# Attention and two feed-forward layers on one core: float32 late scores for five pairs of heads, PSUM banks kept across the stages, and later steps for some loads and stores

## The chip, the cores and the metric

The kernel runs on one core of a Trainium2 chip. The metric is the device time of one execution in microseconds (us). The engines of the core are TensorE (PE in the profile, its weight loads PEld), VectorE (DVE), ScalarE (ACT), GpSimd (POOL) and SyncE (SP), which issues most of the DMAs.

## The reference

Shapes: q, k, v are (4, 8, 576, 64); the first layer is 512 to 2048 to 512, the second too; 2304 tokens.

```python
scores = scale * np.matmul(q, k.transpose(0, 1, 3, 2))     # scale = 1/8
mask = block_i >= block_j                                   # blocks of 64 positions
scores = np.where(mask, scores, -1000000000.0)
attn = softmax(scores)                                      # minus the row's maximum, 1e-9 in the sum
x = (attn @ v) as tokens x 512
h = x @ w_in;  g = np.maximum(h, 0.0) + alpha * np.minimum(h, 0.0);  x = g @ w_out     # first layer
h = x @ w_in2; g = np.where(h > 0.0, h, np.exp(np.minimum(h, 0.0)) - 1.0); out = g @ w_out2
```

The weights arrive as 64-bit floats and are turned into 32-bit ones on the core.

## The kernel before

**Attention** works on 16 pairs of heads, `n` = 0 to 15. A list `SEQ` of 64 slots sets the order: for the first eight pairs the early scores (query rows 0 to 255), one pair a slot, then for each of these pairs three late slots, `i` = 2, 3 and 4 (rows 256 to 383, 384 to 511, and the last 64), then the same for the other eight. Late slots of pairs 0 to 4 are slots 8 to 22. A slot `k` emits, each engine in program order: the scores on TensorE into one of two double banks (`twin`, called pair in the profile), products with v (`second`) and transposes of earlier slots, the row maxima on VectorE (line 319), the exponentials on ScalarE (line 346), and, two slots later, the division by the sums on GpSimd (line 96, tile `p`). The scores of slot `k` + 2 need the double bank of slot `k`, that is, its exponentials.

Early scores multiply float32 tiles as they were loaded (line 290). Late scores are three products of "fp32r" parts: `high_parts` (GpSimd: `qh`, `kh`, `kl`) and `low_parts` (VectorE: `ql`, line 270) split q and k into a high and a low part, and line 297 adds high x high, high x low and low x high. For `i` = 4 the last 64 query rows of both heads stand on the diagonal of a 128 x 128 tile `qdiag` (one for the high and one for the low parts, two sets), which `diagonal` fills by copies on GpSimd and ScalarE, and line 302 multiplies it by both heads' keys, 288 columns at a time.

`second(n, 1)` multiplies five chunks of v with the transposed probabilities `pt` (line 444). The fifth chunk has 64 rows of v, the others 128. Its closure `out` makes the high part of x on ScalarE (line 450) and the low part on VectorE (line 89), for the block of 256 rows and for the 64 tail rows (`xtail`).

**The weights** come by `load_w`: a DMA into `wraw` (three buffers), then, `arrival` ticks later, two steps on ScalarE (133, 134), three on VectorE (138, 139, 143), a word addition on GpSimd (148), a cast on ScalarE (162), a subtraction on VectorE (89, tile `w`). `later(t, f)` emits f after t ticks: a tick is a slot in attention, and half a step afterwards.

**The first layer beside attention** (`l1_beside`, lines 599 and 611) puts six products at a time between slots, for three units of 512 tokens. It borrows PSUM banks of the ring "t" that transposes and `second` use. After attention the steps `units` follow: per step one `f` of 16 columns blocks of the hidden layer, first layer A, B, D (lines 580 and 684), then the second, C (634 and 659). Units 0 to 3 have 512 tokens; unit 4, the 64-row tails of all pairs, has 256. `l1_gate` makes `neg` on ScalarE (557), `g` on VectorE (560), and its high and low parts on ScalarE (564) and GpSimd (89). After attention, all eight PSUM banks are one new pool: "h" takes banks 5, 6, 7, "acc" takes 0 to 4. x goes through DRAM (`xd`), and so does the first layer's output (`zd`, `yd`).

Of the kernel before, what the change touches and what calls it, by code (L numbers as in the profile page):

```python
# [9 lines left out]
F32 = mybir.dt.float32  # L10
# [31 lines left out]
def attention_moe_kernel(ctx: ExitStack, tc: tile.TileContext, qT, kT, v_a, v_b, w1, w2, alpha, out):  # L42
# [146 lines left out]

    att = ExitStack()  # L190
    ps = att.enter_context(pool("ps", 1, space=PSUM))
    twin = [ps.tile([P, 2, 512], F32, name=f"pair{i}") for i in range(2)]
    bank = [None] * 4 + [ps.tile([P, 512], F32, name=f"bank{i}") for i in range(4, 8)]
    ap1 = att.enter_context(pool("att1", 1))
    ap2 = att.enter_context(pool("att2", 2))
    vraws = [ap1.tile([P, 2, 5, D], F32, name=f"vraw{i}") for i in range(2)]

    qdiag = [[ap1.tile([P, P], F32R, name=f"qdiag{i}{k}") for k in range(2)] for i in range(2)]
# [39 lines left out]
    def load_early_v(d):  # L238
        b, hs = duo(d)
        v = vraws[d % 2].rearrange("p h c d -> p (h c d)")[:, :512].rearrange("p (h c d) -> p h c d", h=4, c=2)  # L240
        nc.sync.dma_start(out=v, in_=v_a[b, hs, :, :2, :].rearrange("h p c d -> p h c d"))
        for a in range(2):
            st[2 * d + a]["v"] = v[:, 2 * a:2 * a + 2]

# [7 lines left out]
    def load_late_v(n):  # L252
# [4 lines left out]
        nc.sync.dma_start(out=v[:64, :, 4, :], in_=v_b[b, hs].rearrange("e p d -> p e d"))  # L257

    def high_parts(n):
        s = st[n]  # L260
        q, k = s["raw"]
        for which, x, scale in (("q", q[:, :320], 0.125), ("k", k, None)):
            s[which] = [ap2.tile([P, x.shape[1]], F32R, tag=f"{which}{t}", name=f"{which}{t}") for t in "hl"]
            copy("p", s[which][0], x, scale)
        low_part("p", s["k"][1], k, s["k"][0])

    def low_parts(n):
        s = st[n]
        hi, lo = s["q"]
        dve.scalar_tensor_tensor(out=lo, in0=s["raw"][0][:, :320], scalar=0.125, in1=f32(hi), op0=ALU.mult, op1=ALU.subtract)  # L270

    def diagonal(n):
        for low in range(2):
            for x in range(2):
                r = slice(64 * x, 64 * x + 64)
                copy("pa"[low], qdiag[n % 2][low][r, r], f32(st[n]["q"][low])[r, 256:320])
# [4 lines left out]
    def scores(n, i):  # L281
        s = st[n]
        s["sb", i] = sb = twin[take("s")]
        if i < 4:
# [8 lines left out]
            q0, cols = P * i - 256, slice(0, P * (i + 1))  # L293
            for t, (qp, kp) in enumerate(PASSES):
                for x in range(2):
                    r = slice(64 * x, 64 * x + 64)
                    pe.matmul(sb[:, x, cols], s["q"][qp][r, q0:q0 + P], s["k"][kp][r, cols], start=t == 0, stop=t == 2)  # L297
        else:
            kn = S // 2
            for r in range(2):  # L300
                for t, (qp, kp) in enumerate(PASSES):
                    pe.matmul(sb[:, r, :kn], qdiag[n % 2][qp], s["k"][kp][:, kn * r:kn * (r + 1)],  # L302
                              start=t == 0, stop=t == 2)
# [60 lines left out]
    def transposes(n, i):  # L364
# [3 lines left out]
        if i in (EARLY, 2):  # L368
            s["pt"] = ap1.tile([P, 2, 1280], F32, tag=f"pt{n % 2}", name="pt")
        pt = s["pt"]  # L370
# [48 lines left out]
    def x_out(n, half):  # L419

        b, p = PAIRS[n]
        u = unit_of(n, half)
        if n % (2 * NPAIR) == 2 * NPAIR - 1:
            later(2, lambda: nc.sync.dma_start(out=xd[u], in_=f32(x1[u])))
        if half == 1:
            later(2, lambda: nc.sync.dma_start(out=xd[B][:, :, p, 64 * b:64 * b + 64], in_=f32(st[n]["tail"])))
# [4 lines left out]
    def second(n, half):  # L431
# [8 lines left out]
        for j in chunks:  # L440
            rows = 64 if j == 4 else P
            lo, o = max(0, P * j - q0), place(half, j)
            for x in range(2):
                pe.matmul(op[64 * x:64 * x + 64, lo:qn], s["v"][:rows, x, j, :], s["pt"][:rows, x, o + lo:o + qn],  # L444
                          start=j == 0, stop=j == chunks[-1], skip_group_check=True)
# [209 lines left out]
    def l2_y(u, f, gs):  # L655
        for tg in range(UNITS[u] // P):
# [4 lines left out]
            if f == NF - 1:  # L661
# [5 lines left out]
                else:  # L667
                    for k in range(2):
                        r = S * (2 * tg + k) + 512
                        nc.sync.dma_start(out=out[r:r + 64, :], in_=o[64 * k:64 * k + 64, :])  # L670

# [26 lines left out]
    with tc.manual_schedule(engines={ET.PE, ET.Activation, ET.DVE, ET.Pool, ET.SP}):  # L698
# [31 lines left out]
        for u, a, b, c, d in stretches:  # L730
            assert a >= X_DONE[u]
            parts = l1_beside(u)
            for first, end, n in ((a, b, 2 * FA), (c, d, 2 * KC)):
                slots(k, first)
                k = first
                for j in range(n):
                    next(parts)
                    to = first + (2 * (j + 1) * (end - first) + n) // (2 * n)
                    slots(k, to)
                    k = to  # L740
# [5 lines left out]
    with tc.manual_schedule(engines={ET.PE, ET.Activation, ET.DVE, ET.Pool, ET.SP}):  # L746
# [3 lines left out]
        ps = ctx.enter_context(pool("ps_all", 1, space=PSUM))  # L750
        bank[:] = [ps.tile([P, 512], F32, name=f"bank{i}") for i in range(8)]
        w_pools.append(ctx.enter_context(pool("w2", NF - 8)))
        late_pools.append(ctx.enter_context(pool("late", 1)))
        ring("h", 5, 6, 7)
        ring("acc", *range(5))
        units = [("A", 3), ("A", 4)] + [("B", u) for u in (2, 0, 1)] + [
# [13 lines left out]
        for i in range(len(steps) + lag):  # L770
            if i in w_at:
                arrival[0] = 6 if i < 6 else 4 if i < first_of["C", 2] - 4 else 2
                load_w(*w_at[i])
# [47 lines left out]
```

## Time and profile before

| | |
|---|---|
| median of three runs | 984.5 us (984.43 to 985.5) |
| the profiled execution | 985.47 us; first to last instruction 983.7 us |
| TensorE busy | 959.4 us (98%) |
| VectorE busy | 549.5 us (56%) |
| ScalarE busy | 438.4 us (45%) |
| GpSimd busy | 341.6 us (35%) |
| HBM traffic | 107 GB/s over the span |
| VectorE's first operation | starts at 3.69 us, when the first q has landed |
| one memset of 64 x 128 on VectorE | 0.17 us |

Busy is the union of an engine's instructions. What lies between the profiled execution's time and its span is before the first and after the last instruction. The busy share is a mean over stages that have different limits, so the stages have to be looked at one by one. In the views below a time at a row's start is in us from the first instruction; "idle" and square brackets name the time in which the engine did nothing just before, and what ended it.

### The profile page before, as it was taken

How to read it: one execution, taken by the hardware profiler on the slowest of the kernel's cores; microseconds unless marked ns; L12 is line 12 of the kernel's file. 1: busy time of each engine (PE TensorE's matmuls, PEld its weight loads, DVE VectorE, ACT ScalarE, POOL GpSimd, SP SyncE). 2: the span in 40 equal slices, each digit the busy share in tenths (PEclk: the TensorE clock that was granted, in tenths of full speed). 3: DMA queues.
4: the chain of work that ended last, by engine and by line, in shares of the span. 5: the costliest groups of instructions: out<-in, count | busy, mean ns of one | idle time of the engine just before them, and what ended most of it. 6: DMA issues, size and time to landing. Idle time of an engine off the chain costs nothing.

```text
span 983.7 us, 13873 instructions
## 1 busy us (share of the span) xinstructions
PE 959.4 (98%) x5064; PEld 779.2 (79%) x5064; DVE 549.5 (56%) x1012; ACT 438.4 (45%) x985; POOL 341.6 (35%) x401
## 2 busy tenths in 40 slices
PE   9888999999999999999999999999999999999997
PEld 7556666776789888888888888888888888888896
DVE  6999777775375454543554685994333332433343
ACT  6877787675354443433433553652222222222232
POOL 6888678664264343433443551330000000000000
PEclk9999999999999999999999999999999999999999
DMA  6553574432545522612537444322002100200010
GB/s 197 197 162 95 149 239 161 136 90 94 199 141 175 184 80 85 214 32 97 170 109 244 162 151 150 107 84 109 1 1 86 44 1 0 86 1 1 1 43 22
DMA packets 55524, 105.77 MB, mean 108 GB/s; under 512 B 11040, under 2 KB 29472, under 8 KB 54304
## 3 DMA queue, kind: packets, MB, share of 16 engines
q1 hardware_dynamic: 55168, 104.62, 32.2%
q8 instruction: 40, 0.66, 0.3%
q14 instruction: 28, 0.23, 0.1%
q10 hardware_dynamic: 288, 0.26, 0.1%
HBM read 76.55 MB, written 28.31 MB: 107 GB/s over the span
## 4 chain that ended last, share of the span: by engine, by line
PE 89%; DVE 5%; issue 2%; ACT 2%; POOL 1%; DMA 1%; SPq 0%; POOLq 0%; ACTq 0%; DVEq 0%
PE bank L634 20%; PE bank L659 20%; PE bank L580 16%; PE bank L684 16%; PE bank L444 4%; PE bank L611 3%; PE bank L599 2%; PE bank L384 2%; PE pair L297 1%; PE pair L290 1%; PE bank L377 1%; PE bank L207 1%; PE pair L302 1%; DVE wword L143 1%; DMA wraw<-w 1%
## 5 line engine op out<-in xcount | busy, mean ns | idle before, releaser
L634 PE MATMUL bank<-x,w 128*128 128x512 f32 (+1 forms) x960 | 210.0, 368 | 0.0
L634 PEld LDWEIGHTS bank<-x,w 128*128 128x128 f32 x960 | 169.4, 188 | 31.1
L580 PE MATMUL bank<-x,w 128*128 128x512 f32 (+1 forms) x816 | 175.5, 365 | 3.1 <-DVE g L560 1.9
L580 PEld LDWEIGHTS bank<-x,w 128*128 128x128 f32 x816 | 141.3, 189 | 27.9 <-DVE g L560 2.1
L560 DVE SCALAR_TENSOR_TENSOR g<-neg,beta,bank 128x512 f32<-128x512 f32 (+1 forms) x80 | 55.3, 692 | 130.5 <-ACT neg L557 130.4
L639 DVE TENSOR_SCALAR e<-e 128x512 f32<-128x512 f32 (+1 forms) x80 | 33.6, 420 | 165.5 <-ACT e L638 165.5
L148 POOL TENSOR_TENSOR wword<-wword,wraw 128x512 int32<-128x512 int32 x64 | 92.7, 1448 | 80.8 <-DVE wword L143 60.9
L638 ACT ACTIVATE e<-bank 128x512 f32<-128x512 f32 (+1 forms) x80 | 44.2, 552 | 168.5 <-PE bank L634 168.5
L659 PE MATMUL bank<-w,gs 128*128 128x512 f32 x432 | 104.7, 390 | 0.0
L659 PE MATMUL bank<-w,gsl 128*128 128x512 f32 x432 | 104.7, 390 | 0.0
L96 POOL TENSOR_SCALAR p<-p,stat 128x256 f32<-128x256 f32 (+4 forms) x144 | 85.0, 605 | 31.1 <-DVE stat L355 17.2
L659 PEld LDWEIGHTS bank<-w,gs 128*128 128x128 f32 x432 | 80.6, 188 | 16.3
L659 PEld LDWEIGHTS bank<-w,gsl 128*128 128x128 f32 x432 | 80.6, 188 | 16.3
L557 ACT ACTIVATE neg<-bank 128x512 f32<-128x512 f32 (+1 forms) x80 | 44.0, 550 | 102.6 <-PE bank L580 102.2
L89 POOL TENSOR_TENSOR gs<-g,gs 128x512 fp32r<-128x512 f32 (+1 forms) x46 | 56.5, 1229 | 94.8 <-ACT gs L564 94.8
L346 ACT ACTIVATE p<-pair,stat 128x256 f32<-128x256 f32 (+4 forms) x144 | 77.9, 551 | 24.5 <-DVE stat L319 18.9
L684 PE MATMUL bank<-gs,w 128*128 128x512 f32 (+1 forms) x408 | 87.8, 365 | 0.0
L684 PE MATMUL bank<-gsl,w 128*128 128x512 f32 (+1 forms) x408 | 87.8, 365 | 0.0
L684 PEld LDWEIGHTS bank<-gs,w 128*128 128x128 f32 x408 | 70.7, 189 | 12.2
L684 PEld LDWEIGHTS bank<-gsl,w 128*128 128x128 f32 x408 | 70.7, 189 | 12.2
L143 DVE SCALAR_TENSOR_TENSOR wword<-wraw,wword 128x512 uint32<-128x512 uint32 x64 | 74.3, 1161 | 2.2
L89 DVE TENSOR_TENSOR w<-wword,w 128x512 fp32r<-128x512 f32 x64 | 65.4, 1021 | 15.6 <-ACT w L162 15.4
(82 smaller groups left out, 1249.4 us busy)
## 6 DMA issues: line engine op xcount, KB each, us to landing
wraw<-w SPq DMA_DIRECT2D x64, 512.0 KB, 4.7
xd<-x SPq DMA_DIRECT2D x4, 2048.0 KB, 7.5
x<-xd SPq DMA_DIRECT2D x16, 512.0 KB, 7.0
x<-yd SPq DMA_DIRECT2D x4, 2048.0 KB, 9.5
vraw<-v_a SPq DMA_DIRECT2D x24, 256.0 KB, 3.6
kraw<-kT SPq DMA_DIRECT2D x16, 288.0 KB, 4.5
yd<-gs SPq DMA_DIRECT2D x8, 512.0 KB, 3.4
yd<-gsl SPq DMA_DIRECT2D x8, 512.0 KB, 3.1
```

The costliest lines, as they stand in the source:

```text
L89: return {"v": dve, "p": pool_e}[eng].tensor_tensor(out=out, in0=x, in1=f32(high), op=ALU.subtract)
L96: return pool_e.tensor_scalar(out, x, 1.0 if scale is None else scale, 1.0, ALU.mult, ALU.mult)
L143: dve.scalar_tensor_tensor(out=wi, in0=high, scalar=0xC0000000, in1=wi, op0=ALU.bitwise_and, op1=ALU.bitwise_or)
L148: pool_e.tensor_tensor(out=w, in0=w, in1=units, op=ALU.add)
L346: act.activation(out=out, in_=x, func=AF.Exp, bias=stat[:, k:k + 1], accum_out=stat[:, SUMS + 2 * k:SUMS + 2 * k + 1])
L557: act.activation(out=neg, in_=h, func=AF.Relu, scale=-1.0)
L560: dve.scalar_tensor_tensor(out=g, in0=neg, scalar=beta[:, f:f + 1], in1=h, op0=ALU.mult, op1=ALU.add)
L580: pe.matmul(h, w_in(0, f, wp_, kc), x[:, xp_, kc, :n], start=kc == 0 and t == 0, stop=kc == KC - 1 and t == 2)
L634: pe.matmul(h, w_in(1, f, wp_, kc), x[:, xp_, kc, :], start=kc == 0 and t == 0, stop=kc == KC - 1 and t == 2)
L638: act.activation(out=e, in_=h, func=AF.Exp)
L659: pe.matmul(acc, gs[:, gp_, tg * P:(tg + 1) * P], w_out(1, f, wp_, 0, DM), start=f == 0 and t == 0, stop=f == NF - 1 and t == 2)
L684: pe.matmul(acc, w_out(0, f, wp_, m * P, P), gs[:, gp_, :n], start=first and t == 0, stop=last and t == 2)
```

## The change

It does seven things.

1. Late scores of pairs 0 to 4 (`n < WHOLE`) are one product of the float32 tiles as loaded. GpSimd scales q in place; `kh`, `kl` and `ql` are not made. For `i` = 4 one float32 tile `whole` takes the place of the `qdiag` tiles; all five pairs use the same one.
2. The fifth chunk of v and of `pt` has 128 rows, the lower 64 of them zero. They are zeroed once at the start, so `pt` is now two fixed tiles, and the early v is loaded into the first four chunks by two DMAs instead of one.
3. Banks 4 to 7 stay in a pool of their own over the whole kernel. After attention "h" takes the three of them that were used longest ago, "acc" the fourth and the other banks.
4. At attention's end all slots are done before the last part of `l1_beside`.
5. The write of `xd[3]` is issued 8 ticks after the last pair instead of 2.
6. In steps 52 to 59 `arrival` is 6 instead of 4.
7. The first of the two last output DMAs is issued by ScalarE's queue.

```diff
     att = ExitStack()
+    ps = ctx.enter_context(pool("ps_kept", 1, space=PSUM))
+    bank = [None] * 4 + [ps.tile([P, 512], F32, name=f"bank{i}") for i in range(4, 8)]
     ps = att.enter_context(pool("ps", 1, space=PSUM))
     twin = [ps.tile([P, 2, 512], F32, name=f"pair{i}") for i in range(2)]
-    bank = [None] * 4 + [ps.tile([P, 512], F32, name=f"bank{i}") for i in range(4, 8)]
...
+    pts = [ap1.tile([P, 2, 1280], F32, name=f"pt{i}") for i in range(2)]
+    for i in range(2):
+        dve.memset(vraws[i][64:, :, 4, :], 0.0)
+        dve.memset(pts[i][64:, :, 960:1024], 0.0)
...
+    WHOLE = 5
+    whole = ap1.tile([P, P], F32, name="whole")
+    pool_e.memset(whole, 0.0)
+
     def high_parts(n):
         s = st[n]
         q, k = s["raw"]
+        if n < WHOLE:
+            copy("p", q[:, :320], q[:, :320], 0.125)
+            s["q"], s["k"] = (q[:, :320],), (k,)
+            return
...
     def low_parts(n):
         s = st[n]
+        if n < WHOLE:
+            return
...
     def diagonal(n):
+        if n < WHOLE:
+            for x in range(2):
+                r = slice(64 * x, 64 * x + 64)
+                copy("pa"[x], whole[r, r], st[n]["q"][0][r, 256:320])
+            return
...
-            for t, (qp, kp) in enumerate(PASSES):
+            passes = PASSES if n >= WHOLE else ((0, 0),)
+            for t, (qp, kp) in enumerate(passes):
...
+                if n < WHOLE:
+                    pe.matmul(sb[:, r, :kn], whole, s["k"][0][:, kn * r:kn * (r + 1)], start=True, stop=True)
+                    continue
...
-            later(2, lambda: nc.sync.dma_start(out=xd[u], in_=f32(x1[u])))
+            later(8 if u == B - 1 else 2, lambda t=x1[u]: nc.sync.dma_start(out=xd[u], in_=f32(t)))
...
-            rows = 64 if j == 4 else P
...
-                pe.matmul(op[64 * x:64 * x + 64, lo:qn], s["v"][:rows, x, j, :], s["pt"][:rows, x, o + lo:o + qn],
+                pe.matmul(op[64 * x:64 * x + 64, lo:qn], s["v"][:, x, j, :], s["pt"][:, x, o + lo:o + qn],
...
-                        nc.sync.dma_start(out=out[r:r + 64, :], in_=o[64 * k:64 * k + 64, :])
+                        issue = nc.scalar if tg == 1 and k == 0 else nc.sync
+                        issue.dma_start(out=out[r:r + 64, :], in_=o[64 * k:64 * k + 64, :])
...
                     to = first + (2 * (j + 1) * (end - first) + n) // (2 * n)
+                    if end == LAST and j == n - 2:
+                        to = LAST
...
-        ring("h", 5, 6, 7)
-        ring("acc", *range(5))
+        oldest = rings["t"]
+        ring("h", *oldest[:3])
+        ring("acc", *range(4), oldest[3])
...
-                arrival[0] = 6 if i < 6 else 4 if i < first_of["C", 2] - 4 else 2
+                arrival[0] = 6 if i < 6 or 51 < i < 60 else 4 if i < first_of["C", 2] - 4 else 2
```

GpSimd's order in the late scores of the first pairs, where it prepares pairs 2 and 3, before:

```order
L148 TENSOR_TENSOR wword<-wword,wraw 128x512
L96 TENSOR_SCALAR p_460<-p_460,stat_125 128x384 x2
L96 TENSOR_SCALAR qdiag_117<-qh 64x64 x2
L96 TENSOR_SCALAR qh<-qraw 128x320
L96 TENSOR_SCALAR kh<-kraw 128x576
L89 TENSOR_TENSOR kl<-kraw,kh 128x576
L96 TENSOR_SCALAR p_500<-p_500,stat_126 128x512 x2
L148 TENSOR_TENSOR wword<-wword,wraw 128x512
```

The same place in the changed kernel:

```order
L148 TENSOR_TENSOR wword<-wword,wraw 128x512
L96 TENSOR_SCALAR p_449<-p_449,stat_136 128x384 x2
L96 TENSOR_SCALAR whole<-qraw 64x64
L96 TENSOR_SCALAR qraw<-qraw 128x320
L96 TENSOR_SCALAR p_485<-p_485,stat_137 128x512 x2
L148 TENSOR_TENSOR wword<-wword,wraw 128x512
```

One of two copies into the diagonal tile, and both operations on k, are gone; the rest stands in the same order.

TensorE's order at attention's end (`L611` is the first layer beside attention, `L444` the last `second`, `L580` the first step after attention), before:

```order
L390 MATMUL bank4_103<-ident_75,p4_2824 128x128 x4
L394 MATMUL bank5_104<-ident_75,p4_2824 64x128
L611 MATMUL bank6_105<-gs_2509,w_295 128x512 x3
L611 MATMUL bank6_105<-gs_2584,w_418 128x512 x3
L611 MATMUL bank6_105<-gs_2673,w_505 128x512 x3
L611 MATMUL bank6_105<-gs_2767,w_581 128x512 x3
L444 MATMUL bank7_106<-pt_2899,vraw1_114 64x320 x6
L444 MATMUL bank7_106<-pt_2899,vraw1_114 64x192 x2
L444 MATMUL bank7_106<-pt_2899,vraw1_114 64x64 x2
L580 MATMUL bank5_3004<-x1_2221,w_295 128x512 x12
```

The same place in the changed kernel (`L636`, `L469` and `L605` are the same three lines):

```order
L416 MATMUL bank4_101<-ident_75,p4_2707 128x128 x4
L420 MATMUL bank5_102<-ident_75,p4_2707 64x128
L636 MATMUL bank6_103<-gs_2395,w_306 128x512 x3
L636 MATMUL bank6_103<-gs_2469,w_418 128x512 x3
L469 MATMUL bank7_104<-pt1_119,vraw1_117 64x320 x6
L469 MATMUL bank7_104<-pt1_119,vraw1_117 64x192 x2
L469 MATMUL bank7_104<-pt1_119,vraw1_117 64x64 x2
L636 MATMUL bank6_103<-gs_2558,w_489 128x512 x3
L636 MATMUL bank6_103<-gs_2651,w_548 128x512 x3
L605 MATMUL bank4_101<-x1_2109,w_306 128x512 x12
```

Six products of the first layer now stand between the last `second` and the first step, and that step takes bank 4 instead of bank 5.

ScalarE's order around the second weight of the tails' stage (`neg` starts a step's gate, `L133` and `L134` start a weight), before:

```order
L557 ACTIVATE neg<-bank_3006 128x256
L162 CAST w<-wword 128x512
L564 CAST gsl<-g 128x256
L133 ACTIVATE wword<-wraw 128x512
L134 ACTIVATE wraw<-wraw 128x512
L557 ACTIVATE neg<-bank_3004 128x256
L564 CAST gs<-g 128x256
```

The same place in the changed kernel (`L582` and `L589` are lines 557 and 564):

```order
L582 ACTIVATE neg<-bank_104 128x256
L589 CAST gsl<-g 128x256
L582 ACTIVATE neg<-bank_101 128x256
L162 CAST w<-wword 128x512
L589 CAST gs<-g 128x256
L133 ACTIVATE wword<-wraw 128x512
L134 ACTIVATE wraw<-wraw 128x512
```

The weight's first two steps now stand behind the `neg` ahead of which they stood.

## Rows read from the trace of the kernel before

**Rows 1.** Busy time by stretch: start:end length, each engine's us, granted clock, DMA.

```profile
core 0: us, PE busy (x) PEld busy (x) DVE busy (x) ACT busy (x) POOL busy (x), PEclk, DMA share, GB/s
4.00:24.00 20.00, 19.66 (x163) 15.09 (x162) 14.29 (x45) 14.43 (x63) 12.96 (x28) 1.00 0.65 201
28.50:91.40 62.90, 50.99 (x326) 36.45 (x327) 60.77 (x126) 46.99 (x122) 53.33 (x68) 0.95 0.48 155
91.40:253.40 162.00, 158.50 (x1076) 112.56 (x1075) 113.97 (x289) 110.01 (x312) 104.94 (x157) 1.00 0.44 142
```

**Rows 2.** TensorE's waits from 24 to 98 us: total, times, longest.

```profile
PE bank L390 <- DVE xtail L89: 4.9, 3, 3.2
PE bank L599 <- DVE pt L95: 2.2, 1, 2.2
PE pair L302 <- ACT p L346: 1.9, 1, 1.9
```

**Rows 3.** TensorE in order of time, first step after attention: start, length.

```profile
253.41 1.86 PE L580 MATMUL bank<-x,w 128*128 128x512 f32 x7 [1.27 <-DVE xtail L89]
```

**Rows 4.** All engines in order of time, tails' stage.

```profile
527.39 0.60 SPq L123 DMA_DIRECT2D wraw<-w  x1
...
534.85 0.66 ACT L133 ACTIVATE wword<-wraw 128x512 f32<-128x512 f32 x1 [3.15 <-DMA wraw<-w]
...
535.96 0.36 ACT L557 ACTIVATE neg<-bank 128x256 f32<-128x256 f32 x1
...
536.89 0.96 PE L580 MATMUL bank<-x,w 128*128 128x512 f32 x3 [1.88 <-DVE g L560]
```

**Rows 5.** SyncE's queue in order of time, the end of the kernel.

```profile
979.72 1.20 SPq L670 DMA_DIRECT2D out<-zl  x2
```

**Rows 6.** Groups by line, 28.5 to 78.5 us: count, busy us, mean ns, idle before.

```profile
L270 DVE SCALAR_TENSOR_TENSOR ql<-qraw,qh 128x320 fp32r<-128x320 f32 x4 | 3.2, 808 | 0.0
...
L89 POOL TENSOR_TENSOR kl<-kraw,kh 128x576 fp32r<-128x576 f32 x4 | 5.7, 1423 | 0.3
...
L96 POOL TENSOR_SCALAR qdiag<-qh 64x64 fp32r<-64x64 f32 x8 | 3.6, 448 | 0.3
...
L96 POOL TENSOR_SCALAR kh<-kraw 128x576 fp32r<-128x576 f32 x4 | 2.9, 714 | 0.0
```

**Rows 7.** GpSimd and VectorE in order of time, single instructions.

```profile
38.18 1.40 POOL L89 TENSOR_TENSOR kl<-kraw,kh 128x576 fp32r<-128x576 f32 x1
...
38.82 1.30 DVE L89 TENSOR_TENSOR w<-wword,w 128x512 fp32r<-128x512 f32 x1
...
50.09 1.47 POOL L89 TENSOR_TENSOR kl<-kraw,kh 128x576 fp32r<-128x576 f32 x1
...
50.33 1.79 DVE L143 SCALAR_TENSOR_TENSOR wword<-wraw,wword 128x512 uint32<-128x512 uint32 x1
...
58.98 0.69 DVE L143 SCALAR_TENSOR_TENSOR wword<-wraw,wword 128x512 uint32<-128x512 uint32 x1
...
531.43 0.69 DVE L89 TENSOR_TENSOR w<-wword,w 128x512 fp32r<-128x512 f32 x1 [1.68 <-ACT w L162]
```

**Rows 8.** TensorE in order of time: scores and the work behind them.

```profile
9.17 0.93 PE L290 MATMUL pair<-kraw,qraw 64*128 64x128 f32 x8 [0.31 <-issue]
10.03 0.94 PE L207 MATMUL bank<-qdiag 128*128 128x128 f32 x6
...
65.37 0.30 PE L302 MATMUL pair<-kh,qdiag 128*128 128x288 f32 x1
...
66.17 0.82 PE L384 MATMUL bank<-ident,p 128*128 128x128 f32 x6
...
96.26 0.50 PE L297 MATMUL pair<-kh,qh 64*128 64x512 f32 x2
...
97.15 0.66 PE L390 MATMUL bank<-ident,p 128*128 128x128 f32 x4
```

**Rows 9.** Groups by line over the run: weight loads of `second`.

```profile
L444 PEld LDWEIGHTS bank<-pt,vraw 128*64 128x64 f32 x384 | 24.8, 136 | 23.5 <-issue 6.0 <-DVE stat L319 0.7 <-DVE stat L355 0.5
L444 PEld LDWEIGHTS bank<-pt,vraw 64*64 64x64 f32 x64 | 3.1, 131 | 4.4 <-issue 3.9 <-DMA vraw<-v_a 0.3 <-DMA kraw<-kT 0.3
```

More of the change, by code (lines that the diff above doesn't have):

```diff
@@ L239, in load_early_v @@
         b, hs = duo(d)
-        v = vraws[d % 2].rearrange("p h c d -> p (h c d)")[:, :512].rearrange("p (h c d) -> p h c d", h=4, c=2)
-        nc.sync.dma_start(out=v, in_=v_a[b, hs, :, :2, :].rearrange("h p c d -> p h c d"))
+        v = vraws[d % 2][:, :, :4, :].rearrange("p g (h c) d -> p g h c d", h=2)
         for a in range(2):
-            st[2 * d + a]["v"] = v[:, 2 * a:2 * a + 2]
+            hs = slice(4 * (d % 2) + 2 * a, 4 * (d % 2) + 2 * a + 2)
+            nc.sync.dma_start(out=v[:, a], in_=v_a[b, hs, :, :2, :].rearrange("h p c d -> p h c d"))
+            st[2 * d + a]["v"] = v[:, a]
     def load_late(n):
@@ L293, in scores @@
             q0, cols = P * i - 256, slice(0, P * (i + 1))
-            for t, (qp, kp) in enumerate(PASSES):
+            passes = PASSES if n >= WHOLE else ((0, 0),)
+            for t, (qp, kp) in enumerate(passes):
                 for x in range(2):
                     r = slice(64 * x, 64 * x + 64)
-                    pe.matmul(sb[:, x, cols], s["q"][qp][r, q0:q0 + P], s["k"][kp][r, cols], start=t == 0, stop=t == 2)
+                    pe.matmul(sb[:, x, cols], s["q"][qp][r, q0:q0 + P], s["k"][kp][r, cols],
+                              start=t == 0, stop=t == len(passes) - 1)
         else:
@@ L368, in transposes @@
         if i in (EARLY, 2):
-            s["pt"] = ap1.tile([P, 2, 1280], F32, tag=f"pt{n % 2}", name="pt")
+            s["pt"] = pts[n % 2]
         pt = s["pt"]
@@ L750, in attention_moe_kernel @@
         ps = ctx.enter_context(pool("ps_all", 1, space=PSUM))
-        bank[:] = [ps.tile([P, 512], F32, name=f"bank{i}") for i in range(8)]
+        bank[:4] = [ps.tile([P, 512], F32, name=f"bank{i}") for i in range(4)]
         w_pools.append(ctx.enter_context(pool("w2", NF - 8)))
         late_pools.append(ctx.enter_context(pool("late", 1)))
-        ring("h", 5, 6, 7)
-        ring("acc", *range(5))
+        oldest = rings["t"]
+        ring("h", *oldest[:3])
+        ring("acc", *range(4), oldest[3])
         units = [("A", 3), ("A", 4)] + [("B", u) for u in (2, 0, 1)] + [
```

## The prediction

> **What bounds the kernel now.** I went from the busy time of each engine by stretch, to what ends TensorE's waits, to the single waits in order of time. TensorE is the bound nearly everywhere: in the first 24 us it works 19.66 of 20.00 us, and from 91.4 us to attention's end 158.50 of 162.00 [rows 1]. One stretch differs. From 28.5 to 91.4 us, late scores of the first half with the first layer beside them, TensorE works 50.99 of 62.90 us, so 11.9 us are waits, and its granted clock is 0.95 there, so part of the work ran at the lower of the two levels. VectorE works 60.77 of those 62.90 us. An engine with 2 us of idle time in 63 sets the pace; TensorE's longest waits there end with VectorE's move of a tail, its copy of `pt`, or exponentials that had waited for its maxima [rows 2]. So in this stretch TensorE's own work is cheap and VectorE's dear; elsewhere it is the other way round.
>
> Outside it three waits stand alone: 1.27 us at attention's end [rows 3], 1.88 us at 537 us [rows 4], and the last output DMAs, issued one behind another [rows 5].
>
> **Late scores of pairs 0 to 4.** VectorE loses the `ql` of each pair. Four lie in the stretch, 3.2 us in all [rows 6]; VectorE's recorded instructions overlap a little, so I count 3.0. The first pair's lies before it, where VectorE has idle time (14.29 busy of 20.00 [rows 1]): nothing.
>
> GpSimd loses `kh`, `kl` and half the `qdiag` copies: 2.9 + 5.7 + half of 3.6, or 10.4 us [rows 6]. GpSimd is not what TensorE mostly waits for, but it holds VectorE up. While `kl` ran from 50.09 to 51.56, VectorE's sign step took 1.79 us; alone it takes 0.69. At 38.82 the subtraction for `w` took 1.30 beside another `kl`, against 0.69 alone [rows 7]. That is 1.10 + 0.61 = 1.7 us beside two of the four `kl`. The bounds are 0 (whatever GpSimd does next blocks VectorE just as long) and 10.4 (each freed microsecond had blocked it). I take 2.0, near the 1.7 seen: the other two `kl`, `kh` and the copies add to it, and the `p` products that come forward in their place take most of that back. [...]
>
> TensorE pays. A float32 score of 128 + 256 = 384 columns as the early stage runs it takes 0.86 us to the next work (9.17 to 10.03). The 512-column late score takes 0.89 now (96.26 to 97.15), the two 288-column ones together 0.80 (65.37 to 66.17) [rows 8]. [...]
>
> VectorE's relief is therefore the time saved: 3.0 + 2.0 = **5.0 us**. Half the ScalarE copies into the diagonal tile go as well, but ScalarE works 46.99 of 62.90 [rows 1]: nothing. Next to be late is still VectorE.
>
> **One `whole` for all five pairs** makes the copies into it wait for the last pair's final scores. On ScalarE they stand behind exponentials that need those scores anyway; on GpSimd behind products of older ones. Nothing; without that cover, up to 1 us a pair.
>
> **Last chunk with 128 rows.** The 64-row weight loads are preceded by 4.4 us of idle time, sixteen pairs, 0.28 each; the 128-row loads, issued two at a time, by 23.5 / 192 = 0.12 [rows 9]. With all rows the last chunk's load can run ahead like the others': 0.15 us a pair. Thirteen pairs have their products where TensorE sets the time: **2.0 us**, at most 0.28 x 16 = 4.5, at least nothing. The four memsets lie before VectorE's first work; uncovered they are 4 x 0.17.
>
> **Attention's end.** The first `L580` product waits 1.27 us until VectorE has read the last tail [rows 3], though its bank was not the tail's (the order lists bank5 against bank7) and its first operand, channel block 0 of x, was old. [...] The data of the last pair are needed only nine products later. SP's queue now has loads of x in front of `zd` writes, each waiting for a tail to land; behind them stand z buffers (two). The writes are steps of a stretch apart, so I count nothing; one late buffer would cost 1 to 2 us. The deferred write of `xd3` feeds a unit much later: nothing.
>
> **Tails' stage.** ScalarE's first step on a weight waits 3.15 us for a DMA issued at 527.39, and `neg`, queued behind it, starts at 535.96; hence TensorE's 1.88 us [rows 4]. Two ticks later, one step of f, `neg` stands ahead of that weight. The weights are used a dozen steps on. **1.9 us**; the least is nothing, if the next weight blocks the next `neg`.
>
> **The end.** Two issues for the last tile take 1.20 us on SP [rows 5]; one on ScalarE, beside the other: **0.6 us**. One more v issue for each of the first two double pairs, 0.6 us at most each, delays loads that are used several us later: nothing, else 1.2.
>
> **Sum.** 5.0 + 2.0 + 1.3 + 1.9 + 0.6 = 10.8 us. The profiled execution took 985.47 us, 1.0 above the median, so it would come to 974.7; from the median of 984.5 I forecast **973.7**.
>
> **Rivals.**
> *Stalls move.* GpSimd, freed, starts its word additions and products earlier and meets other SBUF steps of VectorE; only `ql` counts: 3.0 instead of 5.0, 975.7. For: the word additions block too. [...]
> [...]
> [...]
> *An edit does nothing.* Attention's wait may be for x, or the weight's DMA later still: 1.3 to 3.2 less, 975 to 977.
> *Slower.* The clock falls through the whole stretch. After waits of 1.9 and 2.2 us [rows 2] it was at the lower level for a while already. Held there, 50 us of work would take 100: 62.9 + 38, less 5.8, about 1016. It decides from a mean clock of about 0.71, where the stretch grows by 7.8. Against: the early stage, with float32 scores only, ran at 1.00 [rows 1], and the waits shrink.
>
> **Numbers.** Forecast 0.45 (its own range 971 to 976), stalls move 0.18, no relief 0.13, more 0.15, an edit does nothing 0.05, slower 0.04. The range 967.5 to 979.5 takes in all but the last and the far ends of the outer two. About 0.2% (2 us) is what a measurement tells from no change. Unchanged needs no relief and all 4.5 us of float32 passes showing on top with a small edit lost: 0.05 of "no relief". Faster 0.91, same 0.05, slower 0.04.
>
> **What would show it.** In the profile after: VectorE still over 0.9 busy to about 86 us and TensorE's waits there near 4 us; no `ql` of pairs 0 to 4; the sign step never at 1.8 us beside `kl`; float32 scores at 1.0 to 1.1 us; no 64-row weight load; `L580`'s successor starting within 0.2 us of the last `L611` one; no wait of 1.9 near 530; the last DMA issue 0.6 us nearer to the last product. I am wrong if VectorE turns idle in the stretch while TensorE still waits (the pace was not its), or if TensorE waits for GpSimd's word additions instead.

## The result, and the profile after

The changed kernel takes **973.34 us** (median of 4 runs, 972.79 to 973.45) beside 984.46 for the kernel before (983.37 to 985.5): a ratio of 0.9883, 95% interval 0.9871 to 0.9895. The forecast was 973.7. The profiled execution took 972.79 us, its span is 971.0. The span of the one shown of before is 12.8 us longer (983.7; 12.76 before rounding), more than the 11.1 between the medians: that one was 1.0 above its median, this one 0.55 below.

Late scores first: busy time by stretch, from the second late scores of pair 0 to the first of pair 6, after:

```profile
26.00:84.91 58.91, 51.35 (x316) 33.65 (x316) 55.16 (x126) 48.36 (x122) 41.91 (x56) 1.00 0.54 174
```

The same piece of the program before, and in it two stretches in which TensorE's clock was at its lower level (columns as in [rows 1]):

```profile
26.58:92.17 65.59, 53.52 (x343) 37.78 (x343) 62.41 (x131) 49.20 (x127) 55.94 (x70) 0.95 0.50 158
40.80:44.20 3.40, 3.40 (x13) 2.94 (x12) 3.33 (x6) 2.78 (x7) 3.04 (x3) 0.50 0.36 154
54.40:57.80 3.40, 3.40 (x12) 2.09 (x10) 3.37 (x7) 3.40 (x10) 2.31 (x3) 0.51 0.59 188
```

Read these rows as a sum for TensorE. Length less busy time is its waiting: 12.07 us before, 7.56 after. Half of the 6.80 us busy at the lower level, 3.40, is what its own work lost to the clock before; after, the clock never falls in this piece (1.00). What is left is work at full clock: 50.12 before, 51.35 after, which has the float32 products in it. So the piece is 6.68 us shorter: 4.51 of waits and 3.40 of clock, less 1.23 of work.

VectorE's column tells the same 6.68 us in another way. It is busy 62.41 us before and 55.16 after, 7.25 less, and idle 3.18 and 3.75. In the two stretches at the lower level it worked 3.33 and 3.37 of 3.40 us, so it hardly stood still while TensorE ran slowly. The 3.40 is therefore an entry in TensorE's sum, and not yet the time that a steady clock would have saved.

The timed runs bear on that. Each has a mean granted clock over its span; what that lacks to 1, times the span, is what the clock took. The kernel before was timed 41 times beside the experiments. The seven runs at 0.998 have a median of 983.9 us, the 25 at 0.995 and 0.996 one of 984.5: 2 to 3 us more lost to the clock go with 0.6 us of time. A straight line through all 41 has 0.44 us of time for each us of clock, and 0.27 without the two slowest (987.88 and 989.24). At these rates the 3.40 are worth 0.9 to 1.5 us, an estimate; some of the lower clock lies behind the last product (a granted 0.92 from 978.4 to 983.7 us in the profiled execution of before), which blurs it.

Where VectorE's time went, in the same two pieces (columns as in [rows 6]), before and then after:

```profile
L89 DVE TENSOR_TENSOR w<-wword,w 128x512 fp32r<-128x512 f32 x7 | 8.2, 1178 | 0.0
L143 DVE SCALAR_TENSOR_TENSOR wword<-wraw,wword 128x512 uint32<-128x512 uint32 x8 | 7.7, 968 | 0.3
L139 DVE TENSOR_SCALAR wword<-wword 128x512 uint32<-128x512 uint32 x8 | 4.8, 599 | 0.3
L138 DVE TENSOR_SCALAR wword<-wword 128x512 f32<-128x512 f32 x8 | 4.6, 574 | 0.4 <-ACT wword L133 0.4
```

```profile
L143 DVE SCALAR_TENSOR_TENSOR wword<-wraw,wword 128x512 uint32<-128x512 uint32 x8 | 6.5, 811 | 0.3
L89 DVE TENSOR_TENSOR w<-wword,w 128x512 fp32r<-128x512 f32 x7 | 5.5, 781 | 0.0
L138 DVE TENSOR_SCALAR wword<-wword 128x512 f32<-128x512 f32 x8 | 5.4, 677 | 0.8 <-ACT wword L133 0.8
L139 DVE TENSOR_SCALAR wword<-wword 128x512 uint32<-128x512 uint32 x8 | 3.6, 450 | 0.3
```

The steps with two inputs gave back 2.7 us (L89) and 1.2 (L143), those with one input 0.4 together. Four `ql` of the six in the piece are gone, 3.2 us. Summing what every VectorE operation took beyond the shortest of its shape gives 10.6 us before and 4.9 after, so 5.7 us of stalls went, 1.4 of them on `ql`. VectorE is still 0.94 busy (55.16 of 58.91).

The waits that are left, after (columns as in [rows 2]):

```profile
PE bank L416 <- DVE xtail L89: 2.3, 3, 1.6
PE bank L624 <- DVE pt L95: 1.7, 1, 1.7
PE pair L325 <- DVE pair L352: 1.5, 1, 1.5
PE pair L319 <- ACT p L372: 1.3, 2, 0.9
PE pair L325 <- ACT p L372: 0.8, 1, 0.8
```

Attention's end, TensorE in order of time, after: there is no bracket, so no wait; [rows 3] has 1.27.

```profile
239.54 2.28 PE L469 MATMUL bank<-pt,vraw 128*64 128x320 f32 x20
241.75 1.66 PE L636 MATMUL bank<-gs,w 128*128 128x512 f32 x6
243.24 3.11 PE L605 MATMUL bank<-x,w 128*128 128x512 f32 x13
```

The tails' stage, after, where [rows 4] has 1.88, and SyncE's and ScalarE's queues at the end, beside [rows 5]:

```profile
523.12 1.60 PE L710 MATMUL bank<-gsl,w 128*128 128x256 f32 x12
524.56 2.68 PE L605 MATMUL bank<-x,w 128*128 128x512 f32 x11
```

```profile
966.58 0.55 ACTq L696 DMA_DIRECT2D out<-zl  x1
967.27 0.76 SPq L696 DMA_DIRECT2D out<-zl  x1
```

The group of weight loads of the products with v has one form left, all 128 rows [rows 9]:

```profile
L469 PEld LDWEIGHTS bank<-pt,vraw 128*64 128x64 f32 x448 | 29.3, 136 | 26.3 <-issue 6.4 <-DVE stat L381 1.3 <-DVE stat L345 0.7
```

By place, with the working from the starts of the same instructions in both traces:

| place | forecast | between the two traces |
|---|---|---|
| start: the second scores at 8.56 instead of 9.17 | none | 0.6 |
| late scores, 26 to 85 us | 5.0 | 6.7 |
| fifth chunk, from there to attention's end | 2.0 | 1.6 |
| attention's end | 1.3 | 1.3 |
| from the first step to TensorE's last product | 1.9 | 2.3 |
| from that to the last instruction (5.38, now 5.07) | 0.6 | 0.3 |

The first line is not the change: the kernels below have their second scores between 8.4 and 9.2 us, with the same instructions ahead. That difference is taken off where their traces are compared.

### The profile page after: what moved, and what is told of

Same layout as the page of the kernel before. It is cut to its first block, busy times and chain, and to the rows that moved or that the text cites. A ratio compares the mean times of both kernels' runs of the same rounds, so it can differ in the third digit from the quotient of the medians.

```text
span 971.0 us, 13821 instructions
## 1 busy us (share of the span) xinstructions
PE 954.0 (98%) x5034; PEld 774.8 (80%) x5034; DVE 544.9 (56%) x1011; ACT 437.9 (45%) x980; POOL 326.0 (34%) x387
## 4 chain that ended last, share of the span: by engine, by line
PE 91%; DVE 5%; issue 1%; POOL 1%; ACT 1%; DMA 0%; POOLq 0%; ACTq 0%; SPq 0%
PE bank L659 20%; PE bank L684 20%; PE bank L605 17%; PE bank L710 17%; PE bank L469 4%; PE bank L636 3%; PE bank L624 2%; PE bank L410 2%; PE pair L311 1%; PE pair L319 1%; PE bank L403 1%; DVE stat L345 1%; PE bank L212 1%; PE pair L328 1%; DVE wword L143 1%
## 5 line engine op out<-in xcount | busy, mean ns | idle before, releaser
L605 PE MATMUL bank<-x,w 128*128 128x512 f32 (+1 forms) x816 | 175.2, 364 | 0.0
L605 PEld LDWEIGHTS bank<-x,w 128*128 128x128 f32 x816 | 141.3, 189 | 24.5
L582 ACT ACTIVATE neg<-bank 128x512 f32<-128x512 f32 (+1 forms) x80 | 44.1, 552 | 105.8 <-PE bank L605 105.7
L89 POOL TENSOR_TENSOR gs<-g,gs 128x512 fp32r<-128x512 f32 (+1 forms) x46 | 56.2, 1222 | 92.4 <-ACT gs L589 87.4
L143 DVE SCALAR_TENSOR_TENSOR wword<-wraw,wword 128x512 uint32<-128x512 uint32 x64 | 74.9, 1170 | 2.2
L89 DVE TENSOR_TENSOR w<-wword,w 128x512 fp32r<-128x512 f32 x64 | 62.2, 972 | 15.5 <-ACT w L162 15.2
```

What stands on the lines that cost most here:

```text
L89: return {"v": dve, "p": pool_e}[eng].tensor_tensor(out=out, in0=x, in1=f32(high), op=ALU.subtract)
L143: dve.scalar_tensor_tensor(out=wi, in0=high, scalar=0xC0000000, in1=wi, op0=ALU.bitwise_and, op1=ALU.bitwise_or)
L582: act.activation(out=neg, in_=h, func=AF.Relu, scale=-1.0)
L605: pe.matmul(h, w_in(0, f, wp_, kc), x[:, xp_, kc, :n], start=kc == 0 and t == 0, stop=kc == KC - 1 and t == 2)
```

## Experiments

Each is the changed kernel with the edits shown. Times are medians of 4 to 12 runs. The interval of each ratio is about 0.0012 to either side, 1.2 us, so differences under 1 us are read from traces.

**1. The parts again for all pairs.**

```diff
-    WHOLE = 5
+    WHOLE = 0
```

> The changed kernel with the parts again for all pairs (its limit on the pairs set to 0), the other six edits kept. Theory (VectorE set the pace in late scores of the first pairs; the freed instructions are the gain): slower than the changed kernel's 973.3 us by what the slots of the two traces lost between slots 8 and 25, 6.65 us, so 979.3 to 980.5, with the clock at the lower level again somewhere between 38 and 60 us. Rival (the gain between these slots came from the other edits of attention, the fifth chunk or the order of the v loads): at most 2 us slower, 975. By the forecast's own term, 5.0: 978.3.

980.27 us, 6.9 slower (ratio to before 0.9961, 0.9949 to 0.9974). Part 1 of the change is most of the gain, and it is not the other edits' by another name. The piece from 26 us on is again as long as in the kernel before (66.30 us, 65.59 there), and VectorE as busy:

```profile
26.18:92.48 66.30, 52.86 (x344) 38.30 (x344) 62.94 (x131) 49.44 (x128) 56.66 (x71) 0.95 0.49 156
```

The clock was low again for twice 3.4 us, but at 63 and 76 us, not between 38 and 60.

**2 and 3. VectorE's and GpSimd's removed work, each by itself, into tiles that nothing reads.**

```diff
         if n < WHOLE:
+            spare = ap2.tile([P, 320], F32R, tag="ql", name="ql")
+            q, k = s["raw"]
+            dve.scalar_tensor_tensor(out=spare, in0=q[:, :320], scalar=0.125, in1=k[:, :320], op0=ALU.mult, op1=ALU.subtract)
             return
```

> The changed kernel, with one VectorE operation per pair of pairs 0 to 4 of the shape of the removed one (128 x 320, two SBUF inputs), into a tile that nothing reads. Theory: VectorE sets the pace, so four operations of 0.8 us in the stretch cost 3.0 us: 976.3. Rival (the clock or GpSimd alone made the gain, VectorE has slack once kl is gone): under 1 us, 973.3 to 974.3. Rival that VectorE's delays lower TensorE's clock again: over 4.5 us, 978 or more, with a granted clock under 0.97 in the stretch from 28.5 to 86 us.

```diff
             s["q"], s["k"] = (q[:, :320],), (k,)
+            spare = [ap2.tile([P, S], F32R, tag=f"k{t}", name=f"k{t}") for t in "hl"]
+            copy("p", spare[0], k)
+            low_part("p", spare[1], k, spare[0])
             return
```

> The changed kernel, with GpSimd's two operations on k per pair of pairs 0 to 4 (128 x 576 each) done again into tiles that nothing reads. Theory (they hold VectorE up while both work on SBUF): VectorE's sign steps and subtractions rise from 0.69 to between 1.2 and 1.8 us beside them, and 2.0 us are lost, 3.6 at most (6.65 less the 3.0 of ql): 975.3 to 976.9. Rival (whatever GpSimd does next blocks as long): under 0.7 us, 974.0 at most. Rival (GpSimd's own lateness counts): TensorE's waits end with p from GpSimd, over 4 us.

The spare `ql` costs 1.7 us (975.05; 0.9905, 0.9892 to 0.9919), the two operations on k cost **5.5** (978.84; 0.9945, 0.9933 to 0.9958). The forecast had it the other way round, 3.0 and 2.0. The piece from 26 us on, with the spare `ql`:

```profile
26.02:86.45 60.43, 51.41 (x315) 33.69 (x314) 57.35 (x131) 48.31 (x122) 43.23 (x56) 1.00 0.53 170
```

and with the spare operations on k, with its stretches at the lower clock:

```profile
26.57:92.59 66.02, 56.73 (x315) 37.72 (x315) 58.96 (x126) 49.02 (x123) 51.92 (x66) 0.90 0.50 157
39.90:46.70 6.80, 5.44 (x15) 4.34 (x16) 6.58 (x17) 6.14 (x16) 4.68 (x7) 0.50 0.46 193
74.05:80.80 6.75, 5.89 (x17) 4.61 (x18) 5.07 (x14) 3.76 (x10) 6.53 (x7) 0.50 0.46 123
```

`ql` adds 1.46 us of waits (60.43 less 51.41 is 9.02) and nothing else. The operations on k add 1.73 of waits (9.29), and in TensorE's sum the clock, low for 11.33 us of busy time, takes 5.7. VectorE is busy 3.80 us more than in the changed kernel and idle 3.31 more, so its own work does not fill what was lost here.

This execution, in which the piece is 7.1 longer, is the slowest of five (978.1 to 980.5) and the one with the lowest mean clock, 0.993; the fastest has 0.997. So 3.9 us more lost to the clock go with 2.4 us of time. Carried on to the changed kernel's 0.999, that gives about 977: by this estimate, from five runs, 3 to 4 of the 5.5 us are not the clock's.

How the clock's first fall comes about, VectorE, GpSimd and TensorE in order of time:

```profile
34.79 1.40 DVE L138 TENSOR_SCALAR wword<-wword 128x512 f32<-128x512 f32 x1 [0.31 <-ACT wword L133]
...
35.98 1.45 POOL L89 TENSOR_TENSOR kl<-kraw,kh 128x576 fp32r<-128x576 f32 x1
...
36.22 1.50 DVE L139 TENSOR_SCALAR wword<-wword 128x512 uint32<-128x512 uint32 x1
...
41.26 2.26 PE L328 MATMUL pair<-kraw,whole 128*128 128x288 f32 x4 [3.24 <-DVE pair L355]
...
42.77 0.42 DVE L138 TENSOR_SCALAR wword<-wword 128x512 f32<-128x512 f32 x1
...
43.22 0.43 DVE L139 TENSOR_SCALAR wword<-wword 128x512 uint32<-128x512 uint32 x1
```

Two steps that take 0.42 and 0.43 alone took 1.40, beside GpSimd's scaling of q and `kh`, and 1.50, beside `kl`; TensorE waited 3.24 instead of 1.5, and in that wait, at 39.9, its clock fell to 0.50. So one-input steps were held up as well; the prediction had counted only the two-input steps. The row maxima, which read the double banks in PSUM, were not: 128x1024 took 1.23 us beside a word addition and a `p` product (at 41.30), and 1.22 in the kernel before with GpSimd idle (at 227.54). Between before and after, though, it is the two-input steps that gave the time back (3.9 of 4.3 us, the rows above).

**4. Each float32 late score product done twice.**

```diff
-            passes = PASSES if n >= WHOLE else ((0, 0),)
+            passes = PASSES if n >= WHOLE else ((0, 0),) * 2
```

(with start and stop set for both, and the same for i = 4)

> The changed kernel with each late score product of pairs 0 to 4 done twice by TensorE, the second over the first. A late pair of products has 2 x (384 + 512 + 576) = 2944 columns a pair counted once for each head, twice that now. [...] Theory (TensorE had slack, the float32 passes cost nothing while VectorE sets the pace): what exceeds the 7.6 us of waits left shows, about 4 to 6 us, 977 to 979. Rival (TensorE's time shows in full, the waits are VectorE's round trip after each score): 11 to 12 us, 984.5 to 985.5.

977.45 us, 4.1 slower (0.9929, 0.9915 to 0.9942), within the theory's range:

```profile
27.22:89.89 62.67, 62.04 (x371) 40.99 (x370) 53.86 (x126) 48.81 (x122) 40.89 (x55) 1.00 0.52 166
```

TensorE has 62.04 - 51.35 = 10.7 us more work and waits 0.63 instead of 7.56; 6.9 us of the second products lay in former waits. So the 1.2 us of work that came with the float32 products were hidden too.

**5. Experiments 3 and 4 together.**

> GpSimd's two operations on k done again for pairs 0 to 4, and each float32 late score product of these pairs done twice by TensorE: the work of the two runs that took 978.84 and 977.45 us together, more than in either. Theory (the operations hold VectorE up, and that is the whole 5.5 us): VectorE's lateness stays, so at least 978.8. Rival (of the 5.5 us, some 3 are TensorE's clock, which fell in its waits for 2 x 6.83 us): with TensorE kept at work the clock stays at 1.00 and the time is below the 978.84 of the same kernel with less work, 976.5 to 978.

979.09 us (0.9947, 0.9935 to 0.9959), the time of experiment 3 with all of experiment 4's work on top:

```profile
27.23:91.38 64.15, 62.05 (x371) 40.95 (x370) 58.45 (x126) 49.01 (x122) 51.42 (x66) 1.00 0.51 162
```

The total alone fits the first theory, and the rival's 976.5 to 978 was too low. The row fits the rival in part: the clock stayed at 1.00, the waits are 2.10, and beside experiment 4 the operations on k cost 1.6 us, not 5.5. TensorE did 11 us more work than in experiment 3 in the same time, which is only possible because there it stood still or ran at half clock for as long. But the 1.6 is not what the operations cost with a steady clock alone: the second products also fill waits that VectorE's stalls make (VectorE is busy 58.45 us, nearly as in experiment 3), and now TensorE sets the pace. No run holds the clock without adding work, so how the 5.5 divide is not settled.

**6 and 7. Products that nothing reads, put into TensorE's waits** of experiments 1 and 3, to hold the clock. `fill` writes into columns of a double bank that no scores use:

```diff
+        fill(FILL.get(k, 0))
         move = transposes(*transposes_at[k]) if k in transposes_at else None
...
         keep_busy(BUSY.get(k, 0))
+        fill(FILL_END.get(k, 0))
```

> The parts again for all pairs, and 26 products of 128 x 128 on TensorE whose results nothing reads, 8 to 10 each at three places where TensorE stood waiting in that kernel's trace for 1.9 to 2.9 us (before the scores at 39.5 us, before the transposes at 63.0 and 76.2 us). They take about 0.16 us each, 1.3 to 1.6 us a place, inside the wait. Theory (VectorE's and GpSimd's freed work is the gain): no change to the 980.3 of the parts alone, 979.5 to 981. Rival (part of the gain is that TensorE's clock no longer falls after such waits): the clock stays at 1.00, and the time falls by up to half of the two stretches of 3.41 us at the lower level, 1.7 to 3.4 us: 977 to 978.6.

> The changed kernel with GpSimd's two operations on k done again for pairs 0 to 4, as in the run with them alone (978.84), and 14 and 12 products that nothing reads at the two places where TensorE waited there for 3.24 and 2.81 us. In that run two stretches of 6.83 us at the lower clock began in those waits. Theory (the operations hold VectorE up): the loss stays, 978 to 979. Rival (most of the 5.5 us is the clock): the clock stays at 1.00 and only VectorE's own loss is left, 2.0 by the forecast's term: 975 to 976.

984.12 (0.9986, 0.9975 to 0.9996) and 983.25 us (0.9989, 0.9980 to 0.9998), some 4 us slower than without them: outside all expectations. The experiment failed by its own making. In the second:

```profile
41.24 3.39 PE L531 MATMUL pair<-ident 128*128 128x128 f32 x28 [3.17 <-ACT p L375]
44.47 1.14 PE L328 MATMUL pair<-kraw,whole 128*128 128x288 f32 x4
```

They waited for the same exponentials as the scores behind them, though they write other columns, so the wait seems to be on the whole double bank; then they stood in the way for 3.2 us. They say nothing on the clock. Experiment 5 took their place.

**8. Float32 late scores for pairs 0 to 7** (`WHOLE = 8`).

> The changed kernel with float32 late scores for pairs 0 to 7 instead of 0 to 4. Pairs 5 to 7 have their late scores from 82 to 113 us, where the changed kernel's TensorE has no wait over 0.3 us. Theory: TensorE pays there what it hides before, 0.5 us a pair, so 1.5 us slower, 974.8, unless VectorE's waits reach beyond pair 4. Rival (VectorE's relief counts there too): 0.8 us of VectorE a pair, up to 2 us faster, 971.5.

974.92 us, 1.6 slower (0.9898, 0.9886 to 0.9911), as the theory had it: 0.53 a pair. Here the price of a float32 score is seen by itself, first 512 columns in this kernel, then in the changed one:

```profile
89.47 1.13 PE L319 MATMUL pair<-kraw,qraw 64*128 64x512 f32 x4
90.53 0.66 PE L416 MATMUL bank<-ident,p 128*128 128x128 f32 x4
```

```profile
88.86 0.50 PE L319 MATMUL pair<-kh,qh 64*128 64x512 f32 x2
89.75 0.66 PE L416 MATMUL bank<-ident,p 128*128 128x128 f32 x4
```

1.06 us to the next work instead of 0.89.

**9. 64 rows again in the fifth chunk.**

```diff
+            rows = 64 if j == 4 else P
-                pe.matmul(op[64 * x:64 * x + 64, lo:qn], s["v"][:, x, j, :], s["pt"][:, x, o + lo:o + qn],
+                pe.matmul(op[64 * x:64 * x + 64, lo:qn], s["v"][:rows, x, j, :], s["pt"][:rows, x, o + lo:o + qn],
```

> The changed kernel with 64 rows again in the fifth chunk of v. Theory (the 64-row weight load can not run ahead): 0.15 us a pair in the eleven pairs from 85 us on and some in the first five, 1.6 to 2.0 us, so 974.9 to 975.3, and the idle time before the 64-row loads near 0.28 us. Rival (the gain per pair came from another edit, the fixed tiles or the order of loads): no change, 973.3.

975.20 us, 1.9 slower (0.9901, 0.9888 to 0.9914). Nearly nothing of it falls into the late scores of pairs 0 to 4 (0.0 at 85 us), the rest in steps of 0.13 to 0.15 a pair. The 64-row loads are back with their idle time of 4.4 us:

```profile
L470 PEld LDWEIGHTS bank<-pt,vraw 64*64 64x64 f32 x64 | 3.1, 131 | 4.4 <-issue 3.3 <-DMA kraw<-kT 0.6 <-DMA vraw<-v_a 0.3
```

**10. The order at attention's end and the later weight undone; the kept banks stay.**

```diff
-                    if end == LAST and j == n - 2:
-                        to = LAST
...
-                arrival[0] = 6 if i < 6 or 51 < i < 60 else 4 if i < first_of["C", 2] - 4 else 2
+                arrival[0] = 6 if i < 6 else 4 if i < first_of["C", 2] - 4 else 2
```

> The changed kernel with two edits undone that lie far apart in time: all slots before the last part of the first layer beside attention (near 242 us), and the later weight (near 525 us); the kept banks stay. Theory: the weight's part costs 1.9 us again, a wait of 1.9 for g in the tails' stage. At attention's end the kept banks alone remove the wait for the tail's low part: 0 there, 975.2 in all. Rival: the wait was covered by the six products only; it is back with 1.0 to 1.3 us at 243 us, 976.5 in all.

973.34 us, no change (0.9891, 0.9877 to 0.9904). Both edits are worth nothing here. At attention's end the first step follows the last product with v without a wait, so the kept banks alone remove it:

```profile
241.01 2.27 PE L469 MATMUL bank<-pt,vraw 128*64 128x320 f32 x20
243.21 3.02 PE L605 MATMUL bank<-x,w 128*128 128x512 f32 x12
```

The tails' stage is the surprise. ScalarE's order is that of before, but the weight was there:

```profile
522.11 0.66 ACT L133 ACTIVATE wword<-wraw 128x512 f32<-128x512 f32 x1 [0.58 <-DMA wraw<-w]
...
523.24 0.37 ACT L582 ACTIVATE neg<-bank 128x256 f32<-128x256 f32 x1
```

```profile
523.22 1.60 PE L710 MATMUL bank<-gsl,w 128*128 128x256 f32 x12
524.66 1.55 PE L605 MATMUL bank<-x,w 128*128 128x512 f32 x6
```

L133 waits 0.58 for the DMA, not 3.15 [rows 4], and TensorE not at all. The DMA issues of this stage (size of each, median us from issue to landing), before and then here:

```profile
wraw<-w SPq DMA_DIRECT2D x3, 512.0 KB, 7.4
```

```profile
wraw<-w SPq DMA_DIRECT2D x3, 512.0 KB, 5.4
```

and SyncE's queue in order of time, the second and third of these issues, before and here:

```profile
530.27 3.38 SPq L123 DMA_DIRECT2D wraw<-w  x2
```

```profile
520.10 0.91 SPq L123 DMA_DIRECT2D wraw<-w  x2
```

The same transfers, issued in the same order, landed 2 us later in the one profiled execution of before. The first of them took 7.4 us from issue to landing there, and 4.9 to 6.4 in the thirteen traces of the changed kernel and its variants; in none of the thirteen does TensorE wait there. The two kernels compared differ in the other edits too, so whether one of these or the single execution made the transfers late is not shown.

**11. The other two: banks given out as before, the last DMA on SyncE; the order stays.**

```diff
-        oldest = rings["t"]
-        ring("h", *oldest[:3])
-        ring("acc", *range(4), oldest[3])
+        ring("h", 5, 6, 7)
+        ring("acc", *range(5))
...
-                        issue = nc.scalar if tg == 1 and k == 0 else nc.sync
+                        issue = nc.sync
```

> The changed kernel with two other edits undone that lie far apart: after attention the banks are given out as before (5, 6, 7 to h, 0 to 4 to acc), the order at attention's end stays changed; and the first of the last two output DMAs is issued by SyncE again. Theory: six products (1.3 us) now stand between the last product with v and the first step after attention and cover a wait of 1.27, so 0 to 0.3 there; the DMA costs 0.6 by the forecast, 0.3 by the changed kernel's trace: 973.6 to 974.2. Rival (the banks decide): 1.2 us at 243 us, 974.9 to 975.1.

973.66 us (0.9892, 0.9877 to 0.9908), 0.3 slower; 0.65 in the traces, 0.22 of it behind the last product, where SyncE issues both parts again:

```profile
968.24 1.19 SPq L696 DMA_DIRECT2D out<-zl  x2
```

TensorE's order changed with the banks, which was not expected: nine products of the first step run ahead of the last products with v (the second row below), since bank 5 is free by then.

```profile
238.53 1.64 PE L636 MATMUL bank<-gs,w 128*128 128x512 f32 x6
240.00 2.22 PE L605 MATMUL bank<-x,w 128*128 128x512 f32 x9
242.16 2.27 PE L469 MATMUL bank<-pt,vraw 128*64 128x320 f32 x20
```

No wait here either. Either edit alone does; both undone at once, and the later write of `xd3` undone, were not tried.

**12. Ten of VectorE's copies into `pt` moved to ScalarE**, an attempt at a faster kernel.

```diff
             for m, (src, dst) in enumerate(moves):
+                if n < WHOLE and i in (2, 3) and m == 1:
+                    behind.append((src, dst))
+                    continue
...
             exponentials(*here)
+        for src, dst in behind:
+            copy("a", dst, src)
+        behind.clear()
```

> The changed kernel with one of VectorE's two halves of the copies into pt moved to ScalarE, behind the slot's exponentials, for the slots i = 2 and 3 of pairs 0 to 4 (ten copies of 0.4 to 0.5 us). Theory (VectorE still sets the pace up to 80 us): at the ratio of the spare ql (1.7 us for 3.2 us of work) about 2 us faster, 971.3, with TensorE's waits in that stretch down from 7.6 us to 5 or 6. Rival (ScalarE, 46.6 us busy of 57.5, becomes late with the exponentials and the copies): 973.3 or slower, waits that end with p or pt from ScalarE.

973.75 us (0.9895, 0.9881 to 0.9908): no gain.

```profile
26.56:85.05 58.49, 51.37 (x317) 33.68 (x316) 52.40 (x117) 51.29 (x130) 41.50 (x56) 1.00 0.54 174
```

VectorE has 2.8 us less to do, ScalarE 2.9 more, and the piece is 0.4 shorter. So VectorE's throughput alone no longer sets the pace. That the waits left are round trips (scores, maxima, exponentials, next scores), in which ScalarE's added work takes back what VectorE gives, is read from the waits and not tested. No kernel here was faster than the changed one.

## Why the prediction came out right, point by point

The total was right to 0.4 us with terms that were not: the late scores gave 1.7 to 1.9 us more than the sum has, and the tails' stage, 1.9 in the sum, nothing that an experiment could find. That these two cancel is luck.

- **The stage and its bound: right.** The late scores gave 6.7 of the 12.8 us between the traces, and undoing part 1 alone costs 6.9 of 11.1. TensorE's slack hid its added work (experiment 4), and where it has none a pair costs 0.53 (experiment 8, put at 0.5); 512 columns took 1.06 us, within the 1.0 to 1.1 forecast. The 4.5 us of float32 passes that the chances name was the author's estimate and no run shows it; the runs showed 1.23 us more work at full clock in the piece (51.35 for 50.12).
- **"VectorE's relief is therefore the time saved: 3.0 + 2.0 = 5.0": right in what was saved, mis-sized in the 2.0.** VectorE was busy 7.25 us less and the piece became 6.68 shorter. `ql` went as counted (3.2, put at 3.0). The stalls of its other steps fell by 4.3 where 2.0 was put: the forecast had seen 1.7 beside two of the four `kl`, and took the rest to be lost again to the `p` products, which it was not. The sum did not price the clock. It is 3.40 in TensorE's sum and 0.9 to 1.5 by the timed runs.
- **The two halves put back by themselves: 1.7 and 5.5, not 3.0 and 2.0.** The spare `ql` keeps VectorE busy 2.19 us longer, and 1.46 of that end up in TensorE's waits. The operations on k bring stalls and falls of the clock twice as long as those of before (13.6 us for 6.8), so their 5.5 is not their share in the kernel before. How stalls and clock divide the 6.9 of part 1 stays open.
- **TensorE's waits: "near 4 us" left; 7.56 were.** The "near 4" is the author's estimate and rests on no row. The forecast took the gain from waits alone; in TensorE's sum 3.40 of it stands under the clock, so more waits stay. VectorE is over 0.9 busy as said, but experiment 12 shows that this no longer means that its throughput alone sets the pace. The sign step still takes 1.64 us once, beside other GpSimd work.
- **Fifth chunk, 2.0: right**, 1.9 by experiment 9, 0.13 to 0.15 a pair.
- **Attention's end, 1.3: right in size**, the 1.27 of [rows 3]. The kept banks are enough (experiment 10); the six products, 1.49 us from their start to the next work (241.75 to 243.24; the expectation of experiment 11 puts 1.3), are a second cover for the same wait.
- **Tails' stage, 1.9: wrong.** The step that failed is taking [rows 4] for the kernel's habit. With the old step in place and the other edits kept, the wait did not come, and the median did not move. The edit does what was said, against a landing time that this execution alone is shown to have had. How often before's other executions have that wait is open (they were timed, not profiled), and so is whether another edit takes it away.
- **The last DMA, 0.6: half**, 0.2 to 0.3. The second issue on SyncE now takes 0.76, and waits for the copy as before.

Single undoings add up to 6.9 + 1.9 + 0.3 + 0.0 = 9.1; with the 1.3 at attention's end, which two edits cover, 10.4 of 11.1. The last 0.7 is within the intervals, and not settled.

## What to carry to other kernels

Price one engine's stalls beside another over the whole stretch: add up what every step takes beyond the shortest of its shape. Here that gave 5.7 us, where two rows had shown 1.7.

Half of TensorE's busy time at the lower clock (0.50 granted) is what its own work lost, not yet what the kernel lost. In the kernel before, where VectorE worked through those stretches, 0.3 to 0.4 of it reached the time, by the timed runs set against their mean granted clocks.

When a wait ends with a DMA, look whether the same transfer is late in a second execution before an edit is credited with it.

A freed microsecond of a busy engine is not a microsecond of time. For VectorE it was 0.9 in the change (6.68 of 7.25), 0.7 in experiment 2 (1.52 of 2.19), and 0.2 in experiment 12 (0.42 of 2.76), where ScalarE took the work over.

## What the runs showed of the hardware that was not expected

- The clock does not fall with the length of a wait alone. It fell in or just after waits of 1.89, 2.25, 2.88, 2.81 and 3.24 us (before, and experiments 1 and 3), and stayed at 1.00 after 3.20 us (before, at 76.57) and 2.10 (experiment 2). Before it fell after the waits of 1.89 and 2.25 that end at 39.9 and 54.1 us; in experiment 1 the same two waits, ending at 39.5 and 53.7, had no fall. In the late scores of experiments 4 and 5, where TensorE hardly waits, it is 1.00 throughout.
- Transfers of 512 KB, issued in one order, took 7.4 us in the execution of before and 5.4 in that of experiment 10, and one pair of issues on SyncE's queue 3.38 us instead of 0.91. What made the difference is open.
- More work took no more time: experiment 5 (979.09 us) beside experiment 3 (978.84).
